# The second MLP product seeded in its PSUM bank: additions become copies, in a new sequence

## The chip, the cores and the metric

The kernel runs on one core of one Trainium2 chip. The core's engines work side by side and wait for one another by semaphores: TensorE (PE in the profile; PEld are its weight loads), VectorE (DVE), ScalarE (ACT), GpSimd (POOL) and SyncE (SP), which here only issues DMAs. The metric is the device time of one execution in microseconds (us); lower is better. Four runs of the kernel before took 297.83 to 299.12 us, median 298.36.

## The reference

Inputs are q, k, v of shape (8 batches, 8 heads, 576 tokens, 64), omega (128, 64), `w_in` (512, 2048) and `w_out` (2048, 512), all float32. The output is (4608, 512) float32.

```python
def phi(x):                                  # x scaled by 64 ** -0.25
    proj = np.einsum('bhsd,md->bhsm', x, omega)
    h = proj - np.sum(x * x, axis=-1, keepdims=True) / 2.0
    h = h - np.max(h, axis=-1, keepdims=True)
    return np.exp(h) / np.sqrt(m)
kv = np.einsum('bhsm,bhsd->bhmd', phi(k), v)
num = np.einsum('bhsm,bhmd->bhsd', phi(q), kv)
den = np.einsum('bhsm,bhm->bhs', phi(q), np.sum(phi(k), axis=2))[..., None] + 1e-06
x = (num / den).transpose(0, 2, 1, 3).reshape(4608, 512)
h = x @ w_in
out = (h * np.clip(h + 3.0, 0.0, 6.0) / 6.0) @ w_out
```

So: attention in linear form for 8 batches, then a two-layer MLP over all tokens.

## The kernel before

**Stages.** Attention runs batch by batch. For batch b, `load` (line 650) brings in q, k, v: q and k by POOL's DMA queue, cast to bf16, v by SP's. From batch 2 on, DMA transposes on SP's queue (line 801, `Tdma`) make kT and qT. `burst` (lines 820 and 823) then forms the scores of a batch in four score bursts, each a run of 64-row matmuls that takes 4 or 6 PSUM banks; ScalarE takes the exponential of each bank (lines 839 and 847), which frees it. `pair` multiplies kv (1015, 1017) and num (1043), divides (1062 on VectorE, 1066 on ScalarE) into xb, and a transpose (565 in the first two batches, by DMA on SP, line 1098, after that) gives xT.

The MLP works on blocks of 512 tokens, eight of them, and a ninth of the tokens left over. The first product (`mm1` 1122, `mm1_half` 1342, `mm1_quad` 1287) gives h in PSUM, ScalarE and VectorE make g from it (lines 1128/1130, 1323/1325, 1351/1353) into the tile gT. Blocks 1 to 8 then run their second product with `w_out` in `products` (line 1423) as a 2 x 2 block scheme of Strassen's kind with seven products in place of eight: each is 16 matmuls of 256 columns at line 1455, in two halves of 8. Sums of weights (T1, T2, T4 and B12 overwritten) and sums of token blocks (S1 to S4, `combine`, line 1383, on POOL or VectorE) go in.

**What is added up where.** The seven products of a block use three PSUM banks: h0 (products 0 and 1), ha (2, 3 and 5) and hb (4 and 6). TensorE accumulates in a bank, and between two products the bank's state is read out:

- after product 0, h0 is copied to the SBUF tile p1 (line 1482); after product 1, h0 is C11;
- after product 2, u2 = ha + p1; after product 3, u3 = ha + p1; after product 5, C21 = ha + p1;
- after product 4, C22 = hb + u3; after product 6, C12 = hb + u2.

The sums are `plus` (line 1471), VectorE only, 128 x 512 float32. Copies are `evac` (line 550 on ScalarE, 551 on VectorE). A copy or sum must be done before the next product writes the same bank. `store` (line 1551) sends the block's results out by SP's queue (for the last block by SP's or ScalarE's).

**Banks.** PSUM has 8 banks of 512 float32 columns, handed out by `Ring`. A `Virt` is one holding of a bank; `full` says that its owner covers the whole bank, `onto` that it is to be accumulated upon after another engine has written it. If the last holder was not full, `washed` puts a 512-column matmul ahead that covers it. `mm1_quad` and `mm1_pair` work so already.

**The order.** Every engine's instruction order is written out by hand as a list of operation numbers, `ORDER`; `schedule` plays these lists through with planned durations (the constants `SWITCH`, `lat`, `occ`) only to choose a bank for each holding and to work out which semaphores are waited for. An operation that may run on two engines runs on the one whose list names it. The engines take their lists strictly in order, so an instruction that waits holds up all behind it, DMA issues on SP's queue among them.

Filler matmuls ("idle", line 604) keep TensorE at work in the first 20 us.

Of the kernel before, what the change touches and what calls it, by code (L numbers as in the profile page):

```python
# [7 lines left out]
F32 = mybir.dt.float32  # L8
# [5 lines left out]
SWITCH = 0.22  # L14
# [8 lines left out]
        176, 166, 162, 164, 178, 180, 170, 189, 172, 205, 191, 212, 207, 249, 194, 221, 196, 398, 386, 210, 392, 223,  # L23
        237, 399, 199, 387, 244, 228, 393, 239, 226, 388, 242, 394, 231, 400, 252, 389, 395, 401, 404, 407, 215, 247,
        410, 413, 416, 419, 281, 422, 283, 277, 425, 428, 279, 431, 293, 291, 289, 255, 434, 322, 437, 440, 308, 564,
        565, 275, 544, 545, 546, 315, 566, 547, 567, 285, 287, 548, 568, 569, 295, 549, 570, 550, 574, 554, 555, 556,
        551, 575, 576, 557, 571, 558, 577, 348, 578, 335, 350, 353, 559, 337, 340, 374, 579, 379, 376, 361, 560, 580,
        363, 366, 343, 581, 356, 382, 561, 369, 598, 592, 595, 601, 470, 607, 613, 484, 610, 616, 622, 625, 477, 628,
        631, 637, 643, 457, 646, 640, 757, 758, 509, 767, 514, 511, 497, 760, 502, 499, 533, 761, 535, 768, 521, 690,
        538, 523, 526, 770, 771, 670, 773, 776, 777, 683, 774, 794, 697, 788, 791, 818, 797, 843, 806, 823, 822, 820,  # L30
        803, 809, 827, 841, 825, 812, 846, 780, 722, 845, 829, 710, 727, 848, 850, 781, 724, 712, 965, 746, 852, 966,
        734, 715, 975, 751, 968, 736, 981, 976, 739, 748, 969, 978, 979, 878, 982, 984, 985, 891, 988, 989, 898, 996,
        1002, 905, 999, 1005, 1011, 1028, 1026, 1014, 1017, 1031, 1030, 1049, 1051, 1033, 1035, 918, 1020, 1054, 930,
        1037, 920, 942, 923, 1053, 1056, 1058, 1173, 1060, 954, 935, 932, 1174, 944, 947, 1183, 1176, 959, 1177, 1184,
        956, 1099, 1186, 1187, 1086, 1192, 1193, 1113, 1204, 1236, 1207, 1213, 1210, 1106, 1222, 1234, 1259, 1225, 1219,
        1238, 1239, 1257, 1228, 1241, 1189, 1243, 1190, 1262, 1138, 1245, 1261, 1264, 1381, 1196, 1140, 1126, 1268,
        1162, 1143, 1128, 1197, 1266, 1382, 1391, 1150, 1167, 1131, 1164, 1384, 1392, 1385, 1307, 1152, 1155, 1394,
        1395, 1314, 1397, 1400, 1401, 1294, 1398, 1418, 1442, 1430, 1412, 1415, 1421, 1444, 1447, 1446, 1427, 1436,
        1449, 1465, 1433, 1404, 1453, 1451, 1470, 1467, 1405, 1469, 1321, 1346, 1472, 1474, 1589, 1334, 1476, 1590,
        1351, 1339, 1348, 1336, 1358, 1592, 1593, 1515, 1360, 1599, 1600, 1522, 1363, 1370, 1602, 1375, 1372, 1603,  # L40
        1529, 1605, 1608, 1609, 1502, 1606, 1620, 1626, 1623, 1629, 1652, 1635, 1638, 1641, 1650, 1644, 1542, 1654,
        1554, 1655, 1544, 1612, 1556, 1559, 1657, 1547, 1613, 1566, 1659, 1673, 1578, 1571, 1661, 1675, 1568, 1678,
        1677, 1580, 1583, 1700, 1710, 1680, 1682, 1701, 1754, 1731, 1684, 1703, 1704, 1735, 1733, 1758, 1759, 1736,
        1756, 1711, 1761, 1779, 1740, 1738, 1713, 1714, 1777, 1742, 1763, 1719, 1765, 1782, 1781, 1716, 1800, 1717,
        1784, 1805, 1786, 1802, 1788, 1804, 1720, 1723, 1854, 1807, 1856, 1724, 1809, 1811, 1859, 1858, 1823, 1877,
        1879, 1861, 1824, 1863, 1882, 1881, 1826, 1865, 1827, 1884, 1900, 1902, 1886, 1833, 1905, 1904, 1888, 1834,
        1923, 1907, 1909, 1925, 1836, 1911, 1837, 1928, 1839, 1927, 1930, 1946, 1840, 1842, 1934, 1843, 1932, 1846,
        1947, 1847, 1956, 1957, 1949, 1950, 1959, 1960, 1962, 1963, 1966, 1967, 1975, 1981, 1978,
    ],
    "SP": [  # L50
        0, 18, 22, 33, 20, 23, 26, 25, 24, 27, 28, 32, 29, 30, 31, 450, 264, 266, 265, 456, 455, 453, 454, 384, 451,
        452, 553, 667, 666, 563, 669, 573, 668, 583, 663, 517, 505, 541, 529, 664, 542, 665, 874, 779, 875, 1079, 876,
        783, 730, 873, 872, 877, 754, 718, 742, 871, 1084, 755, 991, 1082, 1083, 1080, 1085, 1081, 926, 938, 950, 962,
        987, 963, 1291, 1290, 1195, 1495, 1292, 1199, 1293, 1146, 1170, 1134, 1158, 1289, 1288, 1171, 1287, 1500, 1403,
        1498, 1501, 1499, 1407, 1342, 1354, 1496, 1366, 1378, 1379, 1497, 1550, 1562, 1615, 1574, 1586, 1587, 1611,
        1722, 1726, 1849, 1845, 1973, 1969, 1970, 1974, 1972, 1977, 1980,
# [3 lines left out]
        177, 175, 220, 206, 160, 171, 173, 222, 179, 181, 211, 238, 200, 227, 390, 396, 402, 405, 408, 411, 232, 216,  # L60
        248, 414, 417, 420, 423, 278, 284, 426, 429, 280, 432, 292, 256, 282, 435, 327, 328, 325, 438, 323, 441, 313,
        311, 314, 318, 316, 321, 309, 320, 304, 296, 300, 298, 302, 347, 307, 330, 301, 334, 333, 552, 306, 373, 336,
        360, 355, 381, 383, 357, 599, 582, 593, 596, 602, 471, 475, 473, 608, 476, 487, 614, 490, 611, 617, 489, 485,
        623, 626, 482, 478, 629, 480, 632, 483, 638, 644, 458, 460, 508, 466, 464, 463, 647, 462, 469, 641, 510, 496,
        759, 532, 468, 498, 516, 534, 520, 504, 762, 522, 693, 696, 691, 695, 675, 679, 676, 677, 671, 673, 681, 682,
        688, 684, 686, 689, 795, 703, 698, 789, 700, 819, 792, 702, 798, 844, 807, 709, 824, 821, 804, 810, 830, 842,
        832, 813, 721, 847, 853, 834, 836, 711, 729, 732, 733, 747, 859, 857, 967, 735, 714, 855, 717, 738, 753, 970,
        890, 885, 881, 889, 887, 883, 879, 896, 894, 884, 892, 897, 903, 904, 997, 899, 901, 908, 906, 1000, 1003, 911,
        1006, 917, 1012, 1027, 910, 1029, 1015, 1032, 1018, 1038, 1052, 1050, 1040, 919, 1021, 1055, 931, 1044, 1042,
        1061, 943, 925, 1065, 955, 1067, 1063, 1175, 934, 1178, 1100, 1102, 1104, 1105, 1089, 1095, 1092, 1097, 1093,  # L70
        1098, 1118, 1114, 1205, 1116, 1091, 1237, 1208, 1087, 1214, 1211, 1119, 1109, 1107, 1112, 1235, 1223, 1111,
        1260, 1220, 1240, 1226, 1246, 1121, 1229, 1137, 1258, 1248, 1263, 1125, 756, 1250, 1252, 1269, 1139, 1127, 1273,
        1275, 1163, 1148, 1149, 1271, 1383, 1130, 1151, 1169, 1308, 1312, 1386, 1313, 1310, 1319, 1320, 1315, 1317,
        1303, 1306, 1305, 1299, 1301, 1295, 1443, 1300, 1419, 1297, 1413, 1416, 1431, 1422, 1448, 1445, 1428, 1345,
        1454, 1330, 1466, 1434, 1437, 1460, 1456, 1471, 1468, 1458, 1477, 1324, 1322, 1347, 1326, 1327, 1479, 1335,
        1483, 1357, 1591, 1341, 1481, 1353, 1516, 1520, 1518, 1521, 1371, 1528, 1527, 1523, 1525, 1534, 1530, 1535,
        1532, 1509, 1514, 1505, 1503, 1507, 1511, 1513, 1621, 1508, 1624, 1627, 1538, 1630, 1639, 1636, 1653, 1651,
        1642, 1645, 1543, 1555, 1662, 1656, 1546, 1565, 1549, 1567, 1577, 1664, 1674, 1579, 1668, 1676, 1666, 1679,
        1685, 1585, 1380, 1687, 1702, 1732, 1691, 1689, 1755, 1172, 1705, 1734, 1760, 1737, 1757, 1743, 1745, 1747,
        1588, 1766, 1778, 1749, 1768, 1772, 1770, 1783, 1780, 1789, 1801, 1791, 1795, 1793, 1806, 1812, 1803, 1857,  # L80
        1855, 1816, 1818, 1860, 1814, 1866, 1878, 1880, 1870, 1868, 1883, 1889, 1828, 1901, 1872, 1891, 1903, 1893,
        1906, 1912, 1924, 1914, 1926, 1895, 1918, 1929, 1935, 1916, 1939, 1941, 1948, 1937, 1971, 1983,
    ],
    "DVE": [
        17, 6, 7, 8, 5, 12, 13, 16, 15, 122, 116, 149, 143, 140, 185, 146, 137, 11, 201, 152, 182, 9, 130, 158, 155,
        202, 217, 190, 218, 219, 192, 193, 161, 195, 233, 208, 213, 197, 209, 234, 235, 10, 198, 224, 225, 250, 214,
        229, 245, 240, 241, 230, 243, 246, 253, 254, 391, 397, 403, 409, 406, 652, 251, 415, 412, 653, 418, 654, 421,
        424, 427, 294, 430, 1696, 433, 436, 290, 439, 442, 1697, 584, 312, 319, 276, 286, 288, 585, 317, 310, 1698, 305,
# [335 lines left out]
def _emit(nc, es, q, k, v, omega, w_in, w_out, out):  # L424
# [998 lines left out]
    def products(blk):  # L1423
# [51 lines left out]
        def okeys(i, j):  # L1475
            return [("osb", 2 * i + x, j) for x in range(2)]
# [178 lines left out]
```

## Time and profile before

| | |
|---|---|
| median of four runs | 298.36 us (297.83 to 299.12) |
| the profiled execution | 298.62 us, of which the span is 296.8 |
| granted TensorE clock | 1.00 throughout |
| busy: PE, DVE, ACT, POOL | 289.4, 261.4, 232.4, 187.3 us |
| busy of 30 us from 120 to 150 us: PE, DVE, ACT, POOL | 29.93, 27.40, 26.05, 23.41 us |
| matmuls | 2926, of which 880 at line 1455 and 35 fillers |
| additions at line 1471 | 40 (24 of them u2, u3 and C21), mean 683 to 691 ns |

The span is the time from the first to the last instruction of the program; 1.8 us lie around it. A matmul's own duration (273 ns for 256 columns) is longer than its share of the stream, because matmuls are pipelined: what counts is the time from one start to the next. Bracketed times in a timeline are idle time of that engine before the row, with what ended it. Tile names stand without their numbers, so "p" holds the PSUM banks, p1 and p7, and "u" holds u2 and u3.

### The profile page before, as it was taken

To read this page: it belongs to the slowest core of one execution; us is meant where nothing else is said; L and a number is where in the kernel's file an instruction comes from. 1 tells how busy PE (TensorE), PEld (TensorE's weight loads), DVE (VectorE), ACT (ScalarE), POOL (GpSimd) and SP (SyncE) were. 2 spreads that over 40 slices of the span, in tenths; PEclk is the share of its full clock that TensorE was granted. 3 is DMA by queue.
4 is the path that set the end of the run, shared out by engine and by line. 5 is a ranking of instruction groups with operands and counts; after the bars stand their busy time and mean duration, and the time that the engine had idled before them with its cause. 6 is when DMAs were issued, how large, how long until landed. Compare 5 with 4: busy or idle time off the path is not lost.

```text
span 296.8 us, 7715 instructions
## 1 busy us (share of the span) xinstructions
PE 289.4 (98%) x2926; PEld 218.8 (74%) x2926; DVE 261.4 (88%) x580; ACT 232.4 (78%) x568; POOL 187.3 (63%) x211
## 2 busy tenths in 40 slices
PE   7999999999999999999999999999999999999995
PEld 5768854644785698668857986588759988888884
DVE  4788979799999996899879996998999989999974
ACT  2986888589879987999699887998799877777310
POOL 1666417259669755886699568846789366856310
PEclk9999999999999999999999999999999999999999
DMA  7999999999999999989899799989610620020034
GB/s 223 299 201 194 201 258 137 160 232 160 210 144 197 136 263 207 154 147 206 172 155 134 168 159 224 130 186 146 137 53 18 126 83 0 26 118 2 0 144 141
DMA packets 90100, 44.90 MB, mean 151 GB/s; under 512 B 57936, under 2 KB 87760, under 8 KB 90064
## 3 DMA queue, kind: packets, MB, share of 16 engines
q1 hardware_dynamic: 62640, 31.24, 49.0%
q0 software_dynamic: 26592, 12.46, 33.9%
q10 hardware_dynamic: 832, 0.72, 0.8%
q8 instruction: 23, 0.38, 0.6%
q14 instruction: 13, 0.11, 0.1%
HBM read 36.73 MB, written 9.44 MB: 156 GB/s over the span
## 4 chain that ended last, share of the span: by engine, by line
PE 84%; ACT 7%; DMA 4%; SPq 1%; issue 1%; DVE 1%
PE p L1455 30%; PE p L1287 18%; PE p L1122 14%; PE p L1367 5%; PE p L1342 4%; PE p L1043 3%; PE p L820 3%; PE p L1015 3%; DMA qT<-qb 2%; PE p L823 2%; DMA q<-in_q_dram 2%; ACT tsb L1128 2%; SPq L650 1%; ACT qpT L886 1%; ACT qpT L847 1%
## 5 line engine op out<-in xcount | busy, mean ns | idle before, releaser
L1122 PE MATMUL p<-xT,wi 128*128 128x512 f16 x224 | 52.9, 379 | 0.7 <-DVE xT L551 0.6
L703 DVE TENSOR_REDUCE mx<-kp 128x4 f32<-128x512 bf16 (+1 forms) x79 | 47.6, 626 | 6.6 <-ACT kp L839 4.6
L1325 DVE SCALAR_TENSOR_TENSOR gT<-tsb,p 128x512 f16<-128x512 f16 x72 | 48.3, 690 | 1.8 <-ACT tsb L1323 1.6
L1323 ACT ACTIVATE tsb<-p 128x512 f16<-128x512 f32 x72 | 42.2, 612 | 9.6 <-PE p L1287 6.3
L1455 PE MATMUL p<-wo,gT 128*128 128x256 f16 x368 | 46.3, 273 | 0.0
L839 ACT ACTIVATE kp<-p 128x512 bf16<-128x512 f32 (+1 forms) x70 | 38.0, 579 | 8.9 <-PE p L823 8.9
L847 ACT ACTIVATE qpT<-p 128x512 bf16<-128x512 f32 (+1 forms) x70 | 39.2, 583 | 4.4 <-PE p L823 4.3
L550 ACT COPY p<-p 128x512 f32<-128x512 f32 x61 | 35.5, 598 | 6.7 <-PE p L1287 3.6
L1130 DVE SCALAR_TENSOR_TENSOR gT<-tsb,p 128x512 f16<-128x512 f16 x56 | 36.7, 676 | 2.8 <-ACT tsb L1128 2.1
L1122 PEld LDWEIGHTS p<-xT,wi 128*128 128x128 f16 x224 | 21.0, 98 | 23.9 <-ACT kp L839 1.1
L1455 PEld LDWEIGHTS p<-wo,gT 128*128 128x128 f16 x368 | 35.1, 98 | 4.5 <-issue 0.3
L1383 POOL TENSOR_TENSOR gT<-gT,s 128x512 f16<-128x512 f16 x19 | 22.1, 1162 | 24.1 <-DVE gT L1383 10.6
L1128 ACT ACTIVATE tsb<-p 128x512 f16<-128x512 f32 x56 | 34.0, 638 | 3.0 <-PE p L1122 2.8
L997 POOL TENSOR_TENSOR vc<-v,cc 128x512 bf16<-128x512 f32 (+1 forms) x28 | 28.1, 1003 | 7.9 <-DVE gT L1383 1.3
L1455 PE MATMUL p<-t,gT 128*128 128x256 f16 x256 | 31.1, 273 | 0.0
L1383 POOL TENSOR_TENSOR s<-gT 128x512 f16<-128x512 f16 x19 | 21.9, 1155 | 14.5 <-DVE wo L1383 8.6
L1383 POOL TENSOR_TENSOR gT<-gT 128x512 f16<-128x512 f16 x23 | 26.6, 1157 | 4.9 <-DVE s L1383 3.3
L650 POOL DMA_DIRECT2D qb<-in_q_dram x28 | 19.7, 708 | 13.5 <-PE p L562 10.3
L1455 PEld LDWEIGHTS p<-t,gT 128*128 128x128 f16 x256 | 24.3, 98 | 4.9 <-issue 1.3
L1062 DVE TENSOR_TENSOR xb<-p,rec 128x256 f16<-128x256 f32 (+1 forms) x46 | 20.9, 479 | 0.2
L1383 POOL TENSOR_TENSOR s<-gT,s 128x512 f16<-128x512 f16 x13 | 15.0, 1157 | 9.1 <-DVE s L1383 6.0
L1066 ACT ACTIVATE xb<-p,rec 128x64 f16<-128x64 f32 x82 | 18.8, 358 | 1.3 <-DVE rec L1055 1.1
(140 smaller groups left out, 627.5 us busy)
## 6 DMA issues: line engine op xcount, KB each, us to landing
v<-in_v_dram SPq DMA_DIRECT2D x14, 512.0 KB, 4.9
out_dram<-osb SPq DMA_DIRECT2D x14, 512.0 KB, 4.0
kb<-in_k_dram POOLq DMA_DIRECT2D x14, 256.0 KB, 5.8
qb<-in_q_dram POOLq DMA_DIRECT2D x14, 256.0 KB, 6.4
wo<-in_moe_w_out_dram POOLq DMA_DIRECT2D x8, 256.0 KB, 7.0
wi<-in_moe_w_in_dram POOLq DMA_DIRECT2D x3, 512.0 KB, 7.6
q<-in_q_dram SPq DMA_DIRECT2D x4, 256.0 KB, 4.9
vl<-in_v_dram SPq DMA_DIRECT2D x8, 128.0 KB, 5.5
```

What stands on the lines that cost most here:

```text
L550: return E.copy(dst(), src())
L703: op("DVE", dvet(128 * n), lambda E: E.reduce_max(dst, src, axis=AX.X), p, reads=reads, writes=writes, name="mx" + name)
L839: op("ACT", actt(128 * (d1 - d0)), lambda E, lh=lh, ko=ko, part=part: E.activation(ko, out_of(part, 0, lh)[0].rearrange("p (x m) -> p x m" ...
L847: op("ACT", actt(128 * (d1 - d0)), lambda E, lh=lh, part=part: E.activation(qd[:, part[0]:part[1], lh, :], out_of(part, 1, lh)[0].rearrang ...
L1122: ins = E.matmul(ring.t[vh.slot], wi[:, c, 128 * f:128 * f + 128], xv[:, c, :], start=(c == 0), stop=(c == NJ - 1))
L1128: op("ACT", actt(512), lambda E: E.activation(tsb[tu][:], ring.t[vh.slot], AF.Relu, bias=0.5, scale=1.0 / 6.0), t - 0.1, reads=[vh], write ...
L1130: op("DVE", dvet(512), lambda E: E.scalar_tensor_tensor(gT[gu][:, f, :], tsb[tu][:], 1.0, ring.t[vh.slot], ALU.min, ALU.mult), t - 0.1, re ...
L1287: ins = E.matmul(bank(v)[:, 256 * g:256 * g + 256], w(c, f + g), x[:, c, :], start=start and g == 0 and c == 0, stop=c == 1, skip_group_ch ...
L1323: op("ACT", actt(512), lambda E, v=v, tu=tu: E.activation(tsb[tu][:], bank(v), AF.Relu, bias=0.5, scale=1.0 / 6.0), t - 0.1, reads=[v], wr ...
L1325: op("DVE", dvet(512), lambda E, v=v, tu=tu, dst=dst: E.scalar_tensor_tensor(dst, pieces(tsb[tu][:]), 1.0, pieces(bank(v)), ALU.min, ALU.m ...
L1383: op(engines, {"POOL": 0.157 + n / 475.0, "DVE": 0.08 + n / 2000.0}, lambda E: E.tensor_tensor(dst, x, y, ALU.subtract if minus else ALU.a ...
L1455: ins = E.matmul(ring.t[v.slot][:, 256 * j:256 * j + 256], a[:, f, 128 * j:128 * j + 128], w[:, f, :], start=(first and f == 0 and j == 0) ...
```

## The change

The bank ha is handed out before product 0, together with h0. After product 0, h0 is copied not to the tile p1 but into the bank ha, and products 2, 3 and 5 accumulate on that. So ha holds u2 after product 2, u3 after product 3 and C21 after product 5, and the three additions of p1 become plain copies (`take`), which may run on ScalarE or VectorE. The tile p1 goes. Product 2 now has to wait for the copy into ha; before it began a bank of its own.

The lists in `ORDER` are all new, of the same operations. On TensorE and ScalarE they agree with the old ones in the first 42 and 41 entries. u2, u3 and C21 stand on ScalarE in 16 of 24 cases; p1 stands there in all 8 blocks (7 before), C11 in 7 (6 before). In the other direction, divisions (18 to 10), kvz copies (26 to 19), copies of the quads' p7 (18 to 14) and scalings of v (3 to 1) on ScalarE become fewer. SP's list is changed too: which transposes, loads and stores stand ahead of which. Some planning constants are lower: `SWITCH` (entering a score burst), and `lat` (landing) of loads and of DMA transposes.

```diff
-SWITCH = 0.22
+SWITCH = 0.12
...
 ORDER = {
     "PE": [
         14, 121, 115, 117, 131, 159, 138, 153, 147, 119, 141, 144, 135, 156, 150, 127, 123, 125, 129, 174, 133, 168,
-        176, 166, 162, 164, 178, 180, 170, 189, 172, 205, 191, 212, 207, 249, 194, 221, 196, 398, 386, 210, 392, 223,
+        176, 166, 162, 164, 178, 180, 170, 189, 172, 205, 191, 212, 207, 249, 194, 221, 196, 398, 386, 210, 223, 392,
...
-    p1, u2, u3 = [sbt(x, [128, 512], F32) for x in ("p1", "u2", "u3")]
+    u2, u3 = [sbt(x, [128, 512], F32) for x in ("u2", "u3")]
...
-                       lat=1.4, name="Tdma%s.%d.%d" % (t, b, i), issue=1.5, packet=24.0)
+                       lat=1.0, name="Tdma%s.%d.%d" % (t, b, i), issue=1.5, packet=24.0)
...
-        h0, ha, hb = [Virt(ring, True) for _ in range(3)]
+        h0, ha, hb = Virt(ring, True), Virt(ring, True, True), Virt(ring, True)
...
-        seen = set()
+        seen = {ha}
...
             for h in range(2):
                 def e(E, h=h):
+                    washed(E, ha if n + h == 0 else None)
                     for f in range(4 * h, 4 * h + 4):
...
-                   alloc=[v] if first and h == 0 else [], lat=0.25, name="P%d.%d" % (blk, n))
+                   alloc=[ha, v] if n + h == 0 else [v] if first and h == 0 else [], holds=[ha] if n + h == 0 else [], lat=0.25,
+                   name="P%d.%d" % (blk, n))
...
+        def take(name, v, dst, t, writes):
+            op(EV_O, both(512), evac(lambda: dst, lambda: quarter(v)), t, reads=[v], writes=writes, name="%s.%d" % (name, blk))
+
...
-        op(EV_O, both(512), evac(lambda: p1[:], lambda: ring.t[h0.slot]), t - 0.1, reads=[h0], writes=["p1"],
+        op(EV_O, both(512), evac(lambda: ring.t[ha.slot], lambda: ring.t[h0.slot]), t - 0.1, reads=[h0], writes=[ha],
            name="p1.%d" % blk)
...
-        plus("u2", ha, p1, v2(u2), t - 0.1, ["p1"], ["u2"])
+        take("u2", ha, v2(u2), t - 0.1, ["u2"])
         t = product(3)
-        plus("u3", ha, p1, v2(u3), t - 0.1, ["p1"], ["u3"])
+        take("u3", ha, v2(u3), t - 0.1, ["u3"])
...
-        plus("C21", ha, p1, o(1, 0), t - 0.1, ["p1"], okeys(1, 0))
+        take("C21", ha, o(1, 0), t - 0.1, okeys(1, 0))
```

## The prediction

> **What bounds the kernel now.** I read the busy shares first, then the chain that ended last, then the weight-load waits, then the timeline around each place where TensorE stood still.
>
> ```profile
> PE 289.4 (98%) x2926; PEld 218.8 (74%) x2926; DVE 261.4 (88%) x580; ACT 232.4 (78%) x568; POOL 187.3 (63%) x211
> ...
> PEclk9999999999999999999999999999999999999999
> ...
> PE 84%; ACT 7%; DMA 4%; SPq 1%; issue 1%; DVE 1%
> ```
>
> TensorE is busy 98% of the span at full granted clock and carries 84% of the chain. "Busy" can hide waits, so I split TensorE's time by the start times of neighbouring matmuls in the trace. Dense, a 256-column matmul starts 109 ns after the one before, a 512-column one 216 ns, a 65-column one 29 to 32 ns. From the first matmul (1.46 us) to the start of the last (293.36 us) are 291.9 us: 277.3 us of dense stream (35 filler matmuls among them, 3.8 us), 5.7 us for entering and leaving the 28 score bursts (96 ns before and 108 ns inside each, every time, so 0.204 us each), and 8.9 us of waits. Of the waits 5.2 us lie in the first 24 us and 3.7 us in all the rest. So this change can win little: the two sequences are the same on TensorE until about 19 us, and what lies behind that holds 1.0 + 3.7 = 4.7 us of waits.
>
> The three largest are these. Timeline rows: start, duration, engine, line, instruction, and in brackets the idle time before it and its releaser.
>
> ```profile
> 22.01 0.37 ACT L550 COPY xT<-p 128x256 f16<-128x256 f16 x1 [0.55 <-PE p L565]
> ...
> 22.44 0.39 PE L1342 MATMUL p<-xT,wi 128*128 128x256 f16 x2 [0.46 <-ACT xT L550]
> ```
> ```profile
> 58.39 0.42 DVE L551 COPY xT<-p 128x512 f16<-128x512 f16 x1 [0.32 <-PE p L565]
> ...
> 58.95 1.24 PE L1122 MATMUL p<-xT,wi 128*128 128x512 f16 x5 [0.60 <-DVE xT L551]
> ```
> ```profile
> 178.57 0.68 DVE L1471 TENSOR_TENSOR u<-p 128x512 f32<-128x512 f32 x1
> ...
> 178.85 0.40 PE L820 MATMUL p<-om,kT 64*128 64x128 bf16 x8 [0.44 <-DMA qT<-qb]
> ```
>
> By start times they are worth 0.63, 0.76 and 0.51 us. The additions that the change replaces appear as releasers of TensorE only here:
>
> ```profile
> PEld p L1455 <- DVE u L1471: 1.0, 3, 0.4
> ```
>
> Three waits, 1.0 us in total, but of weight loads, which run ahead: by matmul starts only about 0.2 us of it reached the stream (at 145.2 and 145.8 us). And these are the durations of what is taken away and put in:
>
> ```profile
> L550 ACT COPY p<-p 128x512 f32<-128x512 f32 x61 | 35.5, 598 | 6.7 <-PE p L1287 3.6 <-DVE osb L1471 2.6 <-PE p L1455 0.4
> ...
> L1471 DVE TENSOR_TENSOR u<-p 128x512 f32<-128x512 f32 x16 | 11.0, 687 | 4.5 <-PE p L1455 4.3
> ...
> L550 ACT COPY osb<-p 128x512 f32<-128x512 f32 x8 | 4.8, 600 | 1.8 <-PE p L1455 1.8
> L551 DVE COPY osb<-p 128x512 f32<-128x512 f32 x4 | 2.7, 679 | 0.3 <-PE p L1367 0.3
> ```
>
> A copy saves 0.01 us on VectorE (679 against 687) and 0.09 us on ScalarE (600). The Trainium skill ("ScalarE: Activation LUTs", Step-by-step: what each stage is for) calls PSUM ScalarE's faster destination; these rows show no such difference, and the sum goes by them. The instruction itself is no gain; the freedom to place it on ScalarE, and the new sequence, are what can move the time.
>
> **The change part by part**, in us on TensorE's stream.
>
> 1. *24 additions become copies.* The built order puts 16 of the 24 on ScalarE, 8 stay on VectorE; the p1 copy now goes to PSUM (598 ns, against 600 into SBUF: 8 x 0.002, nothing) and is on ScalarE in all 8 blocks (7 before). To make room the sequence moves other work: 8 divisions (82 pieces of them on ScalarE become 52), 7 small kvz copies (278 ns) and 4 512-wide p7 copies from ScalarE to VectorE, 3 x transposes' copies likewise, 2 vc scalings from ScalarE to POOL. Counted with the mean rows, and ScalarE's pieces at the 0.23 us that 18.8 us for 82 of them give: ScalarE -4.5 us of 232, VectorE -4.4 of 261, POOL +4.8 of 187. None of this is on the path as a sum, since TensorE covers it. It shortens the queues that cause the small waits behind 24 us, which are 3.7 less the two named ones there (1.3) less 0.8 before two score bursts (35.5 and 72.8 us) that stand as they did: 1.6 us. Bounds: all of it gone (-1.6), or as much again because the POOL and VectorE parts come late (+1.6). I take -0.2, since the queue relief is about 2% of the two evacuating engines.
>
> 2. *The seed must survive.* TensorE accumulates on a bank that ScalarE wrote; the code adds a 512-column clearing matmul where the bank's last owner had not covered it. Row for such a matmul: 216 ns, so at most 8 x 0.216 = 1.7. The built order has no 512-column filler matmul, and each line's count of matmuls is unchanged but for one 256-column filler more (36 for 35) in the stretch before 24 us that waits anyway: 0. The Trainium skill ("PSUM — Partial Sum Buffer", Summary: rules for kernel authors) says a seed written by VectorE or ScalarE must be 0, as their writes do not set the accumulate bits; read strictly it asks for the 8 clearing matmuls and 1.7 us, and a seed over cleared bits would be overwritten. No row of this trace shows a bank's bits; the sum goes by the instructions that are there.
>
> 3. *New wait: product 2 behind the p1 copy.* Before, product 2 began a fresh bank and could follow product 0 at once: the work between them is 0.31, 0.43, 0.29, 0.00, 3.48, below nothing, 5.26 and 0.88 us in blocks 1 to 8. Now it must wait for the copy. The chain is 0.16 (a matmul's 273 ns less its 109) + 0.60 + two hand-overs of 0.05 = 0.86. The new sequence puts 1.18, 2.54, 2.83, 0.91, 2.66, 2.63, 3.07 and 1.75 us of other matmuls between. So it is covered in all 8 if ScalarE is free, by only 0.05 in block 4. If the copy stands behind one ScalarE instruction of 0.6, blocks 1 and 4 lose 0.28 + 0.55 = 0.8. Nearest row: product 1 has had the same wait all along, with 0.90 us between in block 5, and p1 is no releaser of TensorE in the waits. Bounds 0 and 0.8; I take +0.1. Behind the waiting product 2 on TensorE stands everything; behind p1 on ScalarE stand the relus and exponentials, as before.
>
> 4. *The bank of ha is held from product 0 on*, some 1 to 3 us longer a block, of 8 banks of which a score burst takes 4 or 6. Nearest rows: weight loads of bursts waited 1.5 and 1.3 us in all for the exponentials that free banks. Bounds 0 and +1.3; I take +0.2.
>
> 5. *SP's queue.* At 171.3 us the qT transpose for batch 6 was issued behind the second output store of block 3, which waits for product 6; it landed 7.4 us later, and the burst waited. In the new order both transposes stand ahead of that store, behind the one that waits for product 4, which ends about 8 us earlier on TensorE. -0.5; next late there are the exponentials, which free banks. For batch 7 it goes the other way: the first kT transpose now comes behind a store that waits for product 6 of block 4 and behind another transpose. By queue steps of 0.55 and 1.4 us and a median landing of 4.3 it lands some 2 us before the first burst that needs it; the slowest landing of the 24 took 7.9, which would cost 1.8. I take +0.1.
>
> 6. *The wait at 22.4 us*: between the transpose and the products that read it stand now two groups of four 65-column matmuls, 8 x 29 ns: -0.2. *The wait at 58.9 us*: four more transposes (0.22) and two 512-column matmuls (0.43) now stand behind the transpose at 58 us, but the last two copies of xT are both on VectorE, one after the other (0.38 more): 0.76 + 0.38 - 0.22 - 0.43 = 0.49, so -0.3. *Block 3's u2*: on ScalarE and with 0.94 us of cover (0.82 before): -0.1.
>
> 7. *The end.* The last 64 KB store moves from SP, where two issues took 1.60 us, to ScalarE's queue (0.55 us an issue). The last one is then issued about 0.3 us earlier: -0.3. Bounds -0.5 and 0.
>
> The planning constants (switch 0.12 for 0.22, smaller landing times) cost nothing themselves: they only steer bank choice.
>
> Sum: -0.2 + 0.1 + 0.2 - 0.5 + 0.1 - 0.2 - 0.3 - 0.1 - 0.3 = -1.2. The profiled execution took 298.62 us, 296.8 of it span; that gives 297.4. It was 0.26 above the median of the four runs (298.36), so against the median I say 297.2 (298.36 - 1.2).
>
> **The rivals.**
>
> *A. The relief counts for more.* Between 60 and 240 us VectorE is about 92% and ScalarE about 88% busy, and most small waits come from their lateness. If all of these go (-1.4 more) and nothing of parts 3 to 5 is lost (-0.4): 295.4. Against: the new order has as many places with under 0.25 us of cover as the old.
>
> *B. The waits move on.* What is gained at 58.9, 178.8 and in the end is lost at the next tight place. Half the gains of parts 5 to 7 (0.7 of 1.4) go: 297.8, no change.
>
> *C. Slower: the p1 copy comes late.* It decides from about one and a half ScalarE instructions ahead of it: with two, blocks 1, 4 and 8 lose 0.88 + 1.15 + 0.31 = 2.3, which makes 298.36 - 1.3 + 2.3 = 299.4; with three, 4.3 and 301.4. For it: of the 7 copies on ScalarE only 2 found it idle (the 0.4 us behind L1455 in the copy's row, two times in ScalarE's waits). Against: product 1 lost nothing by the same copy.
>
> *D. The change doesn't do what it says* (clearing matmuls needed): excluded by the order.
>
> **How the numbers follow.** Forecast 0.45, A 0.20, B 0.15, C 0.20. 0.3% (0.9 us) is about what a measurement of this kernel can tell from no change. The forecast's own range is 296.2 to 298.2; two thirds of it lie at 297.5 or less, beyond -0.9. Faster 0.30 + 0.20 = 0.50; same 0.15 + 0.12 = 0.27; slower 0.03 + 0.20 = 0.23. The range from 295.0 (just past A) to 299.5 (C with two instructions) leaves out about 0.2.
>
> **What would show it.** Right: the wait before the burst near 178 us is gone; no wait of products' weight loads on ScalarE's p1; waits behind 24 us sum to under 3 us; ScalarE's busy time near 228, VectorE's near 257; the last store on ScalarE's queue. Wrong: weight loads of L1456 waiting for ScalarE's copy in blocks 1 and 4, bursts of batch 7 waiting for kT, or new waits on POOL's sums, which got 4.8 us more.

## The result and the profile after

| | before | changed |
|---|---|---|
| median, range, executions | 298.48 us (297.83 to 299.75), 78 | 297.95 us (297.04 to 299.18), 52 |
| ratio, 95% interval | 1 | 0.9983 (0.9976 to 0.9989) |
| profiled execution, its span | 298.62, 296.8 | 297.98, 296.2 |

The change gains 0.53 us (0.18%), where 1.2 were forecast: the sign was right, the size less than half. That is below the 0.3% that the prediction took for what can be told from no change; the interval of the ratio, with 52 and 78 executions, leaves out 1. Ratios here leave out executions at a lower granted clock, and the only trace of e16 below is of such a one (425.5 us, clock 0.66).

The page of the changed kernel: busy shares, TensorE's granted clock, and the chain that ended last.

```profile
PE 290.6 (98%) x2927; PEld 220.4 (74%) x2927; DVE 258.4 (87%) x581; ACT 229.9 (78%) x530; POOL 192.6 (65%) x215
...
PEclk9999999999999999999999999999999999999999
...
PE 90%; ACT 8%; DVE 1%; issue 1%
```

ScalarE (228 expected), VectorE (257) and POOL (192) came out 2, 1 and 0.6 us above what was counted. One matmul more than before is the one filler; no bank was cleared for the seed. DMA is gone from the chain. Now the three places of the prediction in the timeline of the changed kernel (start, duration, engine, line, instruction, and in brackets the idle time before it and its releaser):

```profile
22.41 0.83 ACT L550 COPY xT<-p 128x256 f16<-128x256 f16 x2 [0.41 <-PE p L565]
...
23.30 0.39 PE L1342 MATMUL p<-xT,wi 128*128 128x256 f16 x2 [0.16 <-ACT xT L550]
```
```profile
58.27 0.76 DVE L551 COPY xT<-p 128x512 f16<-128x512 f16 x2 [0.53 <-PE p L565]
...
59.08 1.25 PE L1122 MATMUL p<-xT,wi 128*128 128x512 f16 x5 [0.19 <-DVE xT L551]
```
```profile
178.53 0.40 PE L820 MATMUL p<-om,kT 64*128 64x128 bf16 x8
178.71 0.62 ACT L550 COPY u<-p 128x512 f32<-128x512 f32 x1
```

The idle time in brackets fell from 0.46 to 0.16 and from 0.60 to 0.19, and the burst at 178 us waits for nothing that is shown. The new copies stand in the groups of equal instructions and in the weight-load waits so:

```profile
L550 ACT COPY u<-p 128x512 f32<-128x512 f32 x12 | 7.1, 591 | 12.8 <-PE p L1456 12.8
L551 DVE COPY u<-p 128x512 f32<-128x512 f32 x4 | 2.7, 687 | 0.5 <-PE p L1456 0.4
...
PEld p L1456 <- ACT u L550: 0.9, 3, 0.4
```

No product waits for p1. Three weight loads wait for u2 or u3, 0.9 us, where three waited 1.0 us for the additions before: the copy itself changed nothing there. So far everything looks as forecast. The rest of this document asks where half of the gain went, and starts with what one execution differs from the next.

**Three parts of one execution.** The 113th matmul (at 16.3 to 17.3 us, the same instruction with the same work ahead of it on TensorE in both kernels; the expectations below call it the matmul near 19 us) cuts the time into the start up to it, the stream from there to the start of the last matmul, and the end.

| profile of | time | start | stream | end |
|---|---|---|---|---|
| before, first | 298.62 | 16.60 | 276.75 | 3.45 |
| before, second | 298.01 | 16.46 | 276.25 | 3.46 |
| before, third | 299.04 | 17.18 | 276.59 | 3.46 |
| changed, first | 297.98 | 17.28 | 275.76 | 3.14 |
| changed, second | 297.33 | 16.61 | 275.76 | 3.14 |
| changed, third | 297.08 | 16.35 | 275.77 | 3.15 |
| changed, fourth | 297.14 | 16.43 | 275.77 | 3.14 |
| changed, fifth | 297.39 | 16.69 | 275.76 | 3.13 |

The start is chance. The end is fixed, 0.32 shorter. The changed kernel's stream is the same to 0.01 us five times; the one of before has a best of 276.25 and in two of three profiles something on top (0.50 at 178 us, 0.34 near 130 us). Without the chance parts the change gains 0.49 + 0.32 = 0.81 us, which the fastest executions show too (297.83 against 297.04, 0.79).

### The profile page after: what moved, and what is told of

The parts are those of the page before. It is cut to its first block, busy times and chain, and to the rows that moved or that the text cites. A ratio compares the mean times of both kernels' runs of the same rounds, so it can differ in the third digit from the quotient of the medians.

```text
span 296.2 us, 7705 instructions
## 1 busy us (share of the span) xinstructions
PE 290.6 (98%) x2927; PEld 220.4 (74%) x2927; DVE 258.4 (87%) x581; ACT 229.9 (78%) x530; POOL 192.6 (65%) x215
## 4 chain that ended last, share of the span: by engine, by line
PE 90%; ACT 8%; DVE 1%; issue 1%
PE p L1456 33%; PE p L1287 19%; PE p L1122 13%; PE p L1342 5%; PE p L1367 5%; PE p L1043 3%; PE p L820 3%; PE p L1015 3%; PE p L823 2%; ACT tsb L1128 2%; ACT kp L870 2%; PE p L604 1%; ACT qpT L886 1%; ACT qpT L847 1%; ACT kp L839 1%; PE p L746 1%
## 5 line engine op out<-in xcount | busy, mean ns | idle before, releaser
L1323 ACT ACTIVATE tsb<-p 128x512 f16<-128x512 f32 x72 | 41.6, 610 | 5.9 <-DVE gT L1325 2.9
L550 ACT COPY p<-p 128x512 f32<-128x512 f32 x58 | 33.4, 593 | 10.7 <-PE p L1287 7.4
L847 ACT ACTIVATE qpT<-p 128x512 bf16<-128x512 f32 (+1 forms) x70 | 38.1, 582 | 1.4 <-PE p L823 1.4
L997 POOL TENSOR_TENSOR vc<-v,cc 128x512 bf16<-128x512 f32 (+1 forms) x30 | 30.1, 1003 | 10.4 <-DVE s L1383 3.9
L1128 ACT ACTIVATE tsb<-p 128x512 f16<-128x512 f32 x56 | 33.5, 636 | 4.2 <-PE p L1122 4.1
L1383 POOL TENSOR_TENSOR gT<-gT,s 128x512 f16<-128x512 f16 x23 | 26.9, 1169 | 9.3 <-DVE gT L1325 3.0
L1383 POOL TENSOR_TENSOR gT<-gT 128x512 f16<-128x512 f16 x18 | 20.8, 1155 | 7.9 <-DVE s L1383 3.0
L1383 POOL TENSOR_TENSOR s<-gT,s 128x512 f16<-128x512 f16 x17 | 19.6, 1155 | 7.5 <-DVE gT L1325 3.5
L1383 POOL TENSOR_TENSOR s<-gT 128x512 f16<-128x512 f16 x18 | 20.8, 1155 | 5.3 <-DVE gT L1325 2.2
L1062 DVE TENSOR_TENSOR xb<-p,rec 128x256 f16<-128x256 f32 (+1 forms) x54 | 23.9, 463 | 0.3
L550 ACT COPY u<-p 128x512 f32<-128x512 f32 x12 | 7.1, 591 | 12.8 <-PE p L1456 12.8
```

The source lines that it names most:

```text
L550: return E.copy(dst(), src())
L847: op("ACT", actt(128 * (d1 - d0)), lambda E, lh=lh, part=part: E.activation(qd[:, part[0]:part[1], lh, :], out_of(part, 1, lh)[0].rearrang ...
L1128: op("ACT", actt(512), lambda E: E.activation(tsb[tu][:], ring.t[vh.slot], AF.Relu, bias=0.5, scale=1.0 / 6.0), t - 0.1, reads=[vh], write ...
L1323: op("ACT", actt(512), lambda E, v=v, tu=tu: E.activation(tsb[tu][:], bank(v), AF.Relu, bias=0.5, scale=1.0 / 6.0), t - 0.1, reads=[v], wr ...
L1383: op(engines, {"POOL": 0.157 + n / 475.0, "DVE": 0.08 + n / 2000.0}, lambda E: E.tensor_tensor(dst, x, y, ALU.subtract if minus else ALU.a ...
```

## Experiments

### What each part of the change does

Five kernels put the parts together differently. `e1` has the seed and its copies in before's sequence; `e2` has the changed sequence with the tile p1 and the additions; `e3` is the changed kernel with all 24 copies on VectorE; `e4` is the changed kernel with before's planning constants; `e7` is before with the new constants.

```diff
 e1: kernel before, with the changed functions, and
+move("PE", 1710, 1701)      # product 6.2 behind 6.1
 e2: kernel changed, with before's functions, and the move of e3
 e3: kernel changed, and
+for x, after in ((772, 692), (977, 729), ...):   # 16 operations: u2, u3, C21
+    move("ACT", x, after, "DVE")
 e4: kernel changed, and
-SWITCH = 0.12
+SWITCH = 0.22
 ...
 e7: kernel before, and
-SWITCH = 0.22
+SWITCH = 0.12
 ...
```

> The seed and the three copies in the sequence of before (one product of block 6 moved, since product 2 may no longer stand ahead of the second half of product 0; the copies stay on VectorE where the additions stood). My theory of the new wait: a chain of 0.86 us from product 0 to product 2, so blocks 1, 2, 3, 4 and 6, with 0.31, 0.43, 0.29, 0.00 and 0.00 us of other matmuls between, lose 0.55 + 0.43 + 0.57 + 0.86 + 0.86 = 3.3 us: 1.011 of before. Rival, the copy comes late on a busy ScalarE: half or a whole instruction of 0.6 us more in each of the five, 1.5 to 3 us on top: 1.016 to 1.021. Rival, the wait is absorbed in later slack: under 1 us, 1.003 or less.

> The new sequence without the seed: p1 in its tile again, and u2, u3 and C21 additions on VectorE, 16 of them moved there from ScalarE's list to the place where the plan has them. If the sequence alone makes the gain (transposes earlier on SP, work between, the last store): as the changed kernel, 0.998 of before. If it needs the 16 on ScalarE (my part 1): VectorE gets 16 x 0.69 = 11 us on top of 258, the small waits grow, and it is slower than the changed kernel by 0.5 to 3 us: 1.000 to 1.008.

> The changed kernel with the same 16 copies moved to VectorE, the seed kept. By my part 1 the same as the new sequence with additions, within 0.1%, since a copy there takes 0.679 us and an addition 0.687. If holding the seeded bank from product 0 on, or the wait for the seed, costs something (parts 3 and 4: 0.3 us together), it is that much slower than the new sequence with additions; if the seed itself saves time, faster.

> The changed kernel with the planning constants of before: the same sequence on every engine, other banks in places. My prediction costs them at nothing: 0.998 of before, as the changed kernel. Rival: the bank choice decides waits, and a wait for a bank that another choice would have had free costs some tenths of a us: 0.999 to 1.001.

> The kernel before with the changed kernel's planning constants (switch 0.12, shorter landings): its own sequence and additions, other banks, and one filler matmul less in the start. The changed kernel with the old constants took 1.2 us more than with the new ones, and showed a new wait of 0.99 us at 206 us, of a score burst for the last division that held one of its banks. Theory one (the new constants describe the chip better, so the banks they choose are better for any sequence): about 0.5 us or more faster than before, ratio 0.996 to 0.999. Theory two (a bank choice is better or worse only together with its sequence, by which holding happens to be in the way): the same or slower, ratio 0.999 to 1.004. The prediction's step for the constants (nothing): 0.9995 to 1.0005.

| | seed | sequence | copies on ScalarE | constants | median | ratio, interval | stream | end |
|---|---|---|---|---|---|---|---|---|
| e1 | yes | old | 0 of 24 | old | 304.36 | 1.0194 (1.0178 to 1.0210) | 282.38 | 3.47 |
| e2 | no | new | none | new | 300.32 | 1.0061 (1.0047 to 1.0075) | 278.89 | 3.33 |
| e3 | yes | new | 0 of 24 | new | 299.75 | 1.0038 (1.0026 to 1.0051) | 277.78 | 3.33 |
| e4 | yes | new | 16 of 24 | old | 299.13 | 1.0012 (1.0000 to 1.0025) | 277.83 | 3.15 |
| e7 | no | old | none | new | 298.91 | 1.0016 (1.0006 to 1.0026) | 276.34 | 3.46 |
| changed | yes | new | 16 of 24 | new | 297.95 | 0.9983 (0.9976 to 0.9989) | 275.76 | 3.14 |

Every kernel between the two has a higher median than both. Their profiles say what each lacks, with one reserve: the planner chooses the banks anew for every list, so a kernel with a moved entry has other banks too. Against the changed kernel, 118 of the 328 operations that open a bank holding get another bank in e3, 139 in e4, and e1 and e2 have other banks as well. What a difference of two medians is put down to is therefore only as sure as the wait that its profile shows.

*e1.* The waits of TensorE, and the first of the places (columns of a wait: engine, its line, what released it; us in total, times, longest):

```profile
PE p L1464 <- ACT p L558: 3.0, 5, 1.0
```
```profile
78.86 0.62 ACT L558 COPY p<-p 128x512 f32<-128x512 f32 x1
...
79.53 1.05 PE L1464 MATMUL p<-t,s 128*128 128x256 f16 x8 [0.97 <-ACT p L558]
```

Product 2 now waits for the copy into its bank, in five of the eight blocks. By start times these waits are 1.13, 0.55, 0.52, 0.82 and 0.83 us in blocks 1, 2, 3, 4 and 6, 3.85 in all; the expectation's chain gave 0.55, 0.43, 0.57, 0.86 and 0.86. In block 1, shown above, the copy is late: it starts 0.62 us after product 0 has ended, because it stands in ScalarE's old list behind other work, which waits itself (a cast, 0.35 us for TensorE). In the other four it starts within 0.2 us of the product's end, as in block 4:

```profile
174.84 0.57 ACT L558 COPY p<-p 128x512 f32<-128x512 f32 x1 [0.15 <-PE p L1464]
...
175.47 0.61 PE L1464 MATMUL p<-t,s 128*128 128x256 f16 x4 [0.66 <-ACT p L558]
```

So at product 2 the first theory holds, the chain itself, with one late copy on top. The ratio lies in the rival's range (1.016 to 1.021) for another reason: the stream is 6.13 us longer than before's best, and of the other 2.3 us 1.9 are waits for a kvz copy of ScalarE (0.73 at 172 us) and for VectorE's g (0.58 and 0.59 at 237 and 265 us), whose origin is not shown. The seed's wait is real, and it is the new sequence that covers it.

*e2 and e3.* With all sums or copies on VectorE its queue is late: VectorE is busy 268.8 and 267.7 us, against 258.4 in the changed kernel. The waits of e3, and the place of the largest:

```profile
PE p L1465 <- DVE u L560: 0.8, 1, 0.8
```
```profile
147.71 0.68 DVE L560 COPY u<-p 128x512 f32<-128x512 f32 x1
...
148.45 0.61 PE L1465 MATMUL p<-t,gT 128*128 128x256 f16 x4 [0.78 <-DVE u L560]
```

The same wait stands in e2, for the addition. Copies in place of additions, both on VectorE (e2 to e3), are worth 0.57 us of median, more than the expectation's 0.1%; e2's trace has one wait that e3's lacks (0.78 us at 118.6 us, for a VectorE sum of token blocks), and whether the seed or the other banks removed it is not shown. ScalarE in place of VectorE for 16 of them (e3 to changed) is worth another 1.6 by the ratios. So most of what the seed brings in this sequence is the freedom to place the copies.

*e4.* The constants only choose banks and how many filler matmuls go into the start (39 in e4 and 34 in e7, for 36 and 35), and the prediction put them at nothing. Here is a score burst that has to wait for a bank which the last division (line 1062) still reads; in the changed kernel the same burst has other banks and no wait:

```profile
206.59 0.56 DVE L1062 TENSOR_TENSOR xb<-p,rec 128x384 f16<-128x384 f32 x1
...
207.20 0.40 PE L820 MATMUL p<-om,kT 64*128 64x128 bf16 x8 [0.92 <-DVE xb L1062]
```

This wait and three others (at 65, 182 and 186 us) cost this execution 2.0 us. The one at 182 us (0.43) is not one for a bank: it goes back to a DMA transpose of xT that landed late, after 5.8 us. Other executions of the same kernel were up to 0.97 faster, although no start seen is earlier than its 16.33: not all four waits come every time. By the ratios the old constants cost 0.9 us (0.0029 of 298.5). In before's sequence (e7) the new constants move the stream by 0.09 over before's best only, and the median is 0.53 higher. So no set of banks is better by itself: it fits a sequence or not, and theory one of e7's expectation is out.

### What is fixed and what is chance

> The changed kernel once more, unaltered, for a second profile. In its first profile the waits up to 24 us summed to 5.78 us, in the one of before to 5.21, in the five kernels with the new sequence or the seed to 4.67 to 5.38, although up to about 19 us all have the same instructions; behind 24 us the waits were 2.62 us against 3.69. Theory one (the start is chance: it differs from execution to execution, and the rest is fixed by the sequence): behind 24 us the waits are again 2.4 to 2.8 us, the wait before the burst at 178 us is absent again, and the start lies anywhere from 4.6 to 5.9, the execution's time moving with it (297.0 to 298.2 us). Theory two (the start is longer with this sequence, and its gain is given back there): 5.5 us or more up to 24 us again.

> The kernel before once more, unaltered, for a second profile. If the wait of 0.51 us at 178 us (qT landing 7.4 us after its issue, where 4.3 is the median) is fixed by the order of SP's queue, it is there again, within 0.2 us; if the slow landing was chance, it is absent and the waits behind 24 us sum to 3.2 us instead of 3.7. The start up to 24 us lies anywhere from 4.6 to 5.9 us by theory one (chance), near 5.2 or less by theory two (the changed kernel's start is longer because of its sequence).

> The changed kernel unaltered, a third profile. In two profiles the stream from the same matmul near 19 us to the last one took 275.76 and 275.76 us and the tail 3.14, against 276.25 and 276.75 (a late transpose landing in the second) and 3.46 of before: a fixed gain of 0.81 us, which the fastest executions show too (297.04 against 297.83), while the medians differ by 0.53 only. Theory one (the missing 0.28 is the chance start, at 16.3 to 17.3 us for the same matmul in both kernels): stream 275.7 to 275.8 again. Theory two (the changed kernel has chance waits of its own behind 19 us, such as the 0.57 us that the version with the late transpose showed at 182 us): stream of 276.0 or more in some executions.

> The kernel before unaltered, a third profile. If the late landing near 178 us is rare, the stream is 276.2 to 276.3 us again with no wait at 178 us; if it comes often, it is there again and the stream about 276.7. The start lies anywhere from 16.3 to 17.3 us.

> The changed kernel unaltered, a fourth profile. Three profiles gave the stream from the same matmul near 19 us to the last one as 275.76, 275.76 and 275.77. Theory one (only the start is chance): 275.75 to 275.80 again, with the start anywhere from 16.3 to 17.4. Theory two (chance waits behind 19 us): over 276.0 in this profile or the next.

> The changed kernel unaltered, a fifth profile; as for the fourth. If neither shows a stream of over 276.0, chance waits of this kernel are not what the medians' missing 0.28 us shows, as far as five profiles can tell.

The numbers are in the table of the three parts above. The second and third profile of before decide the largest term of the prediction. Its timeline at the burst where the first profile had shown the wait for qT, and the landing of that transpose as the DMA view gives it (issued at 171.20, from issue to landing):

```profile
178.21 0.40 PE L820 MATMUL p<-om,kT 64*128 64x128 bf16 x8
```
```profile
DMA to landing us min/median/max: 5.8/5.8/5.8
```

Same place in the queue, issue within 0.13 us of the first profile, landing after 5.8 us in place of 7.4, no wait. In the third profile it landed after 6.7 and no wait stood there either. Against the start of its burst it came 1.2 and 0.3 us early in these two; in the first profile the burst had waited 0.51 for it. The order of SP's queue had put the transpose at the edge; what made it late was one slow landing. (The 4.3 us that the expectation calls the median is that of the kT transposes; the twelve qT ones of the first profile have 5.4.)

Theory two of the changed kernel's start (its gain given back there) is out: its starts of 16.35 to 17.28 cover those of before.

### The transposes on SP's queue

```diff
 e8: kernel changed, and
+move("SP", 1293, 1199)      # qT of batch 6 behind the second store of block 3
 e16: kernel before, and
+move("SP", 1199, 1293)      # that store behind qT of batch 6
```

> The changed kernel with one entry of SP's list moved: the first qT transpose of batch 6 stands again behind the second output store of block 3, which waits for product 6, as it did before. Nothing else differs. Theory of the prediction (step 5): the transpose is issued some 6 us later, lands after its burst is due, and the burst near 178 us waits again: 0.4 to 0.6 us more on the stream at that place and a ratio some 0.0015 to 0.002 higher than that of the changed kernel, thus about 1.000. Rival (the 7.4 us landing was chance, or the cover is long enough): no wait there, time as the changed kernel, 0.998.

> The kernel before with one entry of SP's list moved: the second output store of block 3 stands behind the qT transpose of batch 6 and no longer ahead of it, so that the transpose is issued some 4 to 6 us earlier. Nothing else differs. Theory of the prediction (step 5: the late transpose costs 0.5 us): about 0.5 us faster, ratio 0.998. Theory after the second and third profile of before (the wait came from one slow landing and is absent in most executions): same to 0.1 us faster, ratio 0.9995 to 1.0005.

e8: 297.72 us, ratio 0.9983 (0.9971 to 0.9994), the changed kernel's own. The transpose (the second of the batch's two, not the first) went out at 171.46, landed after 5.5 us, and TensorE waited for nothing near 178 us. But the late transpose did cost its profiled execution, the slowest of 12, 0.50 us by another way (stream 276.33). POOL's next load of q overwrites the tile that the transpose reads:

```profile
177.94 0.79 POOL L658 DMA_DIRECT2D qb<-in_q_dram  x1 [2.44 <-DMA qT<-qb]
```
```profile
183.12 0.28 PE L1464 MATMUL p<-t,gT 128*128 128x256 f16 x1 [0.43 <-POOL gT L1391]
```

The load waited 2.44 us for the landing, and the sums behind it in POOL's list came late; the one that TensorE needs at 183 us came 1.65 us later than in the changed kernel's first profile, held up on the way by VectorE's sums too. In the changed kernel's five profiles this load does not wait. e16: 298.31 us, ratio 0.9998 (0.9988 to 1.0008). So by the medians moving the transpose is worth nothing that 10 or 12 executions can show, in either kernel, and the wait at 178 us did not come back. "Nothing else differs" is not quite so: the planner also gave other banks to 43 of 328 operations in e8 and to 68 of 336 in e16. What settles step 5 is the unaltered kernel's second and third profile.

### The end, and the cover of product 2

```diff
 e9: kernel changed, and
+move("ACT", 1983, 1980, "SP")    # the last 64 KB store
 e10: kernel changed, and
+move("ACT", 759, 468)            # p1 of block 1
+move("ACT", 1383, 1130)          # p1 of block 4
 e15: kernel changed, and
+move("DVE", 383, 378, "ACT")     # last copy of xT near 58 us
```

> The changed kernel with its last 64 KB store issued from SP's queue again, behind the store that stands there, as in the kernel before; nothing else differs. From the last matmul's start to the end of the execution the changed kernel took 3.13 us, before 3.45, in two profiles each within 0.02. Theory (step 7 of the prediction: the queue of the last store is worth 0.3): the tail is again 3.4 to 3.5 us and the time 0.3 above the changed kernel's, ratio 0.9990 to 0.9998. Rival (the tail is shorter because of what the last copies run on, not of the queue): tail 3.1 to 3.2, ratio 0.998.

The timeline of e9's end, and of the changed kernel's:

```profile
292.89 0.55 ACTq L1548 DMA_DIRECT2D out_dram<-osb  x1
...
293.40 1.25 SPq L1548 DMA_DIRECT2D out_dram<-osb  x2
```
```profile
292.86 1.40 ACTq L1540 DMA_DIRECT2D out_dram<-osb  x2
...
293.36 0.60 SPq L1540 DMA_DIRECT2D out_dram<-osb  x1
```

With two stores on SP the last one ends its issue 0.39 us later (294.65 against 294.26), the end is 3.43 us in place of 3.14, and the median 298.19, 0.24 above the changed kernel's (ratio 0.9993, 0.9980 to 1.0006, which also covers the changed kernel's). Stream 275.77: nothing else moved, and no bank differs. By the trace step 7 holds.

> The changed kernel with the p1 copy moved later in ScalarE's list in two blocks: in block 1 behind a small scaling and an exponential (about 0.7 us), in block 4 behind a group of divisions (0.7 to 1.4 us). Nothing else differs. Step 3 of the prediction gave a chain of 0.86 us from product 0 to product 2 against a cover of 1.18 us in block 1 and 0.91 in block 4. If that working is right, product 2 waits 0.3 to 0.5 us in block 1 and 0.6 to 1.4 in block 4, 0.9 to 1.9 us in all, ratio 1.001 to 1.005, and the releaser of those waits is ScalarE's copy into PSUM. Rival (product 2 hides more than was worked out, or a wait there is given back at the next one): under 0.3 us, ratio 0.998 to 0.999.

The move was larger than the expectation says: counted in ScalarE's list, p1 of block 1 went behind five instructions, and started at 79.91 in place of 77.67; that of block 4 went behind a group of divisions that itself waited 1.69 us for VectorE's reciprocals. 303.09 us, ratio 1.0164 (1.0143 to 1.0184), and these waits of TensorE:

```profile
PE p L1465 <- ACT p L559: 3.5, 2, 2.0
```

By start times product 2 lost 2.16 us in block 1 and 1.69 in block 4; the stream's other 1.2 us lie in further waits (0.38 near 89 us, 0.27 and 0.42 near 109), which may also come from the banks, 104 of them different here. In block 1 the copy ended 2.27 later (80.51 for 78.24), of which 0.08 is this execution's later start; 2.16 of the other 2.19 reached TensorE. So its slack in the changed kernel was about 0.03 us, where the working (1.18 of cover less a chain of 0.86) had given 0.32. The chain is as described; the slack is gone because the copy starts when ScalarE's list lets it, at 77.67, 0.36 us after product 0 has ended.

> The changed kernel with one copy moved: the last copy of xT near 58 us runs on ScalarE, which stands idle there, as it did in the kernel before, and no longer on VectorE behind the other one. Nothing else differs. In the changed kernel the two copies ran one after the other on VectorE from 58.27 to 59.03, and TensorE waited 0.36 us. By the rows ScalarE's copy of 512 columns takes 0.58 and would end at 58.85. Theory of the prediction's step 6 (the two copies in a row on VectorE cost part of the gain): the wait falls to about 0.18, the stream by 0.1 to 0.2 us, ratio against before 0.9970 to 0.9985. Rival (another operand is late next): wait and stream as they are.

297.91 us, ratio 0.9989 (0.9980 to 0.9998), stream 275.81 against 275.76; the wait is 0.41 against 0.36. The copy on ScalarE could start only at 57.62, behind the transposes that it reads (VectorE's began at 57.40), and with 0.58 us it ended 0.04 later than the second copy on VectorE would have. The rival holds: what bounds this place is the last transposes and one copy behind them, not the row of two on VectorE.

## Why the prediction was right or wrong

**The step that failed is 5, "SP's queue": -0.5, with +0.1 against it.** It took the wait at 178 us for a property of the order, because the profile named a DMA and the diff moved that DMA forward. It was one landing of 7.4 us in one execution; before's two other profiles (5.8 and 6.7 us) have no wait there, and moving the transpose alone (e8, e16) moves no median. Worse, the sum was then taken off the median: the profiled execution carried a chance wait of 0.5 us, and taking a chance wait of one execution off a median counts a gain that two of the three profiled executions never had to give. The text noted itself that this execution was 0.26 us above the median. Of the 0.67 us by which the forecast missed, 0.4 are this step; the rest, 0.28, stays open below. Without the step the sum is -0.8, and the fixed parts measured are -0.81. That these agree so closely is luck: the other terms measured come to -1.25, and 0.45 of losses that nobody foresaw bring them back. Rival B's 297.8 (by its own terms 297.9), too, is near the measured 297.95 without its mechanism: the gains at 58 us and at the end stayed, and the one at 178 us had mostly not been there to lose.

The other terms, by the second profiles of both kernels (waits by start times):

| term | predicted | measured |
|---|---|---|
| 1, queue relief | -0.2 | waits at 35, 54 and 73 us 0.11, 0.12 and 0.05 shorter, a new one of 0.17 at 162 us: about -0.1 |
| 2, clearing matmuls | 0 | none |
| 3, wait behind p1 | +0.1 | 0, but with some 0.03 us of slack in block 1 |
| 4, bank held longer | +0.2 | no wait of its own found in the stream; the bursts' weight loads waited 2.0 + 1.3 us for exponentials, 1.5 + 1.3 before |
| 5, SP's queue | -0.4 | 0 |
| 6, 22 us | -0.2 | 0.63 to 0.32: -0.31 |
| 6, 58 us | -0.3 | 0.76 to 0.36: -0.40 |
| 6, block 3's u2 | -0.1 | a wait of 0.12 at 145 us is gone |
| 7, the end | -0.3 | -0.32 |
| not foreseen | | 19 to 21 us: waits of 0.36 become 0.55, and one filler of 0.11 |
| constants | 0 | nothing themselves, but the banks they choose are worth 0.9 us here (e4) |

The waits listed fall by 0.75 us, the filler takes 0.11 back; the stream's -0.49 leaves +0.15 to waits under 0.06 us that aren't listed one by one. For step 6 the size came out near although the reason for 58 us was wrong in part (e15).

Step 3 had the right mechanism, and the wait that it shares with rival C was the true danger of this change: e1 pays 3.85 us at product 2 and 5.8 in all, e10, with late copies, 4.7 against before. The changed sequence was laid so that it is covered, by less than was worked out. One row was read too simply there: the 598 ns of "p<-p" mix 36 copies into banks with 25 into the SBUF tiles p1 and p7. Counted off in the order of ScalarE's list, the p1 copy took 587 ns into SBUF before (7 copies) and 578 into the bank after (8), 0.07 us in all: still nothing for the sum.

In step 2 the prediction read 8 clearing matmuls, 1.7 us, out of the Trainium skill ("PSUM — Partial Sum Buffer", Summary: rules for kernel authors). The page's row says that such a seed must be 0, since the bits ignore ScalarE's and VectorE's writes; it names no clearing matmul. Here the seeds are not 0 and the products are added onto them as written; the matmul count (2927, one filler more) shows that the kernel has no clearing matmul, and no such cost appears.

**What stays open.** The fixed gain is 0.81, the medians differ by 0.53 (interval of the ratio: 0.33 to 0.72 us). The missing 0.28 must lie in parts that vary: chance waits that the changed kernel has more of, or later starts. None of its five profiles shows such a wait, and their starts are not later than before's. But all five took 297.98 us or less, and the times of the other executions say more: with the latest start of any trace (17.35) and its stream of 275.77 the changed kernel would take 298.07 us, and 19 of its 52 executions took longer, up to 299.18. For before the same sum with its best stream is 298.87, and 14 of 78 lie above. So in over a third of the changed kernel's executions something comes late that none of its profiles caught. A candidate, not tested, stands near 182 us, where TensorE needs VectorE sums that stand behind one that waits for an xT transpose. In the five profiles that transpose landed after 2.8 to 4.5 us and TensorE did not wait; in e4, with the same lists, it landed after 5.8 and TensorE waited 0.43, in e2 after 5.6 and 0.25. e7 has the same riddle: 0.09 in the stream, 0.53 in the median. What the executions without a profile do differently was not settled.

## What to carry to other kernels

A wait that a profile puts down to a DMA landing may be a draw and not a constant: profile the same kernel again before crediting a change with its removal, and never take one execution's chance wait off a median. An accumulator seeded from another engine turns a vector addition into a copy that ScalarE can take as well, but puts a copy between two matmul groups: here it paid only with the sequence laid anew around that copy, and the copy's place in its engine's list was the thing to count. Where a planner gives out PSUM banks, its constants belong to the sequence they were chosen with; carry over both or neither. And compare the banks of two variants before putting their difference down to the line that was moved: moving one or two entries changed none of 328 in e9 and 104 in e10.

## What the runs showed of the hardware that was not expected

The start of an execution is a matter of chance worth 1.0 us, at a granted clock of 1.00 in the page's rows. The first matmuls (256 columns) come 213 ns apart, then at 109 ns; where the step falls differs. The timelines of the changed kernel's first and third profile:

```profile
4.99 2.83 PE L746 MATMUL p<-identf,k 128*128 128x128 f32 x14
```
```profile
4.99 1.90 PE L746 MATMUL p<-identf,k 128*128 128x128 f32 x14
```

The same 14 transposes, behind the same work, take 2.83 or 1.90 us, and the 113th matmul starts at 17.28 or 16.35. In 17 of the 18 traces of this study (all but e16's) it lay between 16.33 and 17.35. The step is not all of it: in before's first profile these transposes ran at 109 ns, and the 113th matmul still started at 16.60. In a kernel whose stream is the same to 0.01 us from one execution to the next, this start alone makes two profiles differ by more than the change is worth.

Landing times vary as much: the same transpose at the same place landed after 7.4, 5.8 and 6.7 us in three executions of one kernel.
